# Linear attention's KV sums on 32-column tiles, and KV folded into wo on sixteen 32x32 tiles

## The chip, the cores and the metric

One core of one Trainium2 chip runs the kernel. The metric is device time in microseconds (us) of one execution. "Before" took 845.64 us (median of four runs, 845.39 to 847.52) in the rounds in which the change was timed.

Engines: PE does the matrix products (PEld is its weight load, which overlaps the products: busy 388.2 us beside PE's 838.6 in a span of 843.5), DVE is the vector engine, ACT the scalar engine, POOL the general engine, SP issues transfers (DMA). PE writes to PSUM, which this kernel uses as eight buffers of 512 f32 numbers (2 KB) a partition, called banks here; DVE and ACT copy from there.

## The reference, cut to what matters

```python
qkv = (x @ wqkv) ...                         # S = 2048, D = 1024, H = 32 heads of Dh = 32
pq, pk = phi(q), phi(k)
kv  = einsum('bhsd,bhse->bhde', pk, v)       # one 32x32 matrix a head
z   = einsum('bhsd->bhd', pk)
num = einsum('bhqd,bhde->bhqe', pq, kv)
den = einsum('bhqd,bhd->bhq', pq, z)[..., None] + 1e-06
o   = num / den
return o.transpose(...).reshape(B, S, D) @ wo
```

A layer norm with modulation stands ahead of it, and a gated MLP (D = 1024, F = 3584) follows and takes most of the time. The change touches `kv`, `z` and the product of `kv` with `wo`.

## The kernel before

Tokens go in four blocks (`sc`) of 512, each of four tiles (`t`) of 128. Four heads share one 128-column group `hg`; there are eight groups. The KV sum of block `sc-1` is taken in the middle of the K projection of block `sc`:

```python
    def kv_phase(sc):
        for hg0 in range(0, HG, 3):
            nh = min(3, HG - hg0)
            kvp = acc_b("kvp")                              # one PSUM bank
            kvv = kvp[:, 0:3 * (P + 1)].rearrange("p (g e) -> p g e", e=P + 1)
            for i in range(nh):
                for t in range(STC):
                    mm(kvv[:, i, :], lhsT=pks[sc][:, t, (hg0 + i) * P:(hg0 + i + 1) * P],
                                     rhs=vs[sc][:, t, hg0 + i, 0:P + 1], start=(t == 0), stop=(t == STC - 1))
            # DVE adds kvv to kv_acc

    for sc in range(NSC):
        if sc > 0:
            k_phase(sc, 0, 2)
            kv_phase(sc - 1)
            if sc >= 2:
                row = mod_rows(blks)                        # "modr": modulation rows, already 128x32-tiled
            k_phase(sc, 2, 4)
            # ... rest of K, V, layer norm of the next block
```

Each product is 128 by 129 (128 columns of V and a column of ones for `z`), although only the four 32x32 blocks on its diagonal are wanted. The rest is masked away, the result is transposed group by group, and wo is multiplied by it ahead of time ("fold"), so that later one product does both steps:

```python
    # after the last kv_phase: KVZ = kv_acc * kvmask (block-diagonal), Zden from z
    q_phase(1, 2, 4)
    tpk = acc_b("tp", (HG, P), BF16)
    for hg in range(HG):
        transpose(tpk[:, hg, :], KVZ[:, hg, :])
    # ... copies to KVT, den_sum(0), den_spread(0)
    q_phase(1, 4, 5)
    wf = [(hg, nb) for hg in range(HG) for nb in range(NNB)]
    for qc in range(5, 11):
        q_phase(1 + qc // 8, qc % 8, qc % 8 + 1)            # one Q chunk: 8 matmuls, then phi on ACT and DVE
        for hg, nb in wf[3 * (qc - 5):3 * (qc - 4)]:
            ps = acc_b("wf")
            w = wo[hg // 4][:, hg % 4, nb * NB:(nb + 1) * NB]
            mm(ps[:], lhsT=KVT[:, hg, :], rhs=w, start=True, stop=True)
            nc.scalar.copy(out=w, in_=ps[:])
```

PSUM is used from two pools of four banks: `acc_a` for the dense products, `acc_b` for everything else, so kvp, modr, tp, den, wf and the output projection (`a_ps`) share four banks.

## Time and profile before

| Part of PE's time | Read from | us |
|---|---|---|
| whole span of the profiled run | first line of the page | 843.5 |
| PE busy | part 1 | 838.6 |
| four KV sums | chain of waits, four pieces | 7.26 |
| fold into wo | chain of waits, six pieces | 3.47 |
| eight transposes of KV | chain of waits | 0.45 |

The page of the kernel before: the first line and part 1 give busy time and share of the span, and the last line here, from part 4, gives the shares of the chain that ended last.

```profile
span 843.5 us, 10565 instructions
...
PE 838.6 (99%) x4312; PEld 388.2 (46%) x4312; DVE 307.8 (36%) x604; ACT 173.8 (21%) x267; POOL 55.7 (7%) x160
...
PE 99%; DVE 0%; ACT 0%; issue 0%
```

PE is the bound, all the way through (busy for 99% of the span, and 99% of the chain). So only what leaves PE's stream can be gained, and whatever makes PE wait is lost.

The chain of waits of the kernel before, in order of time. Columns: start in us, length in us, what, number of instructions.

```profile
65.29 1.81 PE kvp L98 x32
...
94.73 1.81 PE kvp L98 x32
96.55 1.84 PE modr L98 x32
...
126.98 1.82 PE kvp L98 x32
128.80 1.84 PE modr L98 x32
...
158.77 1.82 PE kvp L98 x32
...
164.04 0.45 PE tp L101 x8
...
168.61 0.65 PE wf L98 x3
...
180.48 0.22 PE wf L98
```

The KV sums (kvp) take 1.81 us each, 57 ns a matmul. Two of them are followed by modr. The fold (wf) is 0.65 us for three matmuls, 216 ns each.

A piece of the chain starts with its first matmul, so the delay between kinds of matmul falls into the piece ahead of it. This delay is called the **drain** below: in the trace of the changed kernel the first matmul on smaller tiles came 93 ns late, and the first whole-array matmul after them 95 to 102 ns late (start of the next matmul, less the columns of the last). For comparisons below I use **sections**: from the end of the dense product ahead (start of its last matmul plus 216 ns) to the start of the next dense matmul. They are computed from the matmul starts in the trace.

### The profile page before, as it was taken

How to read it: one execution, taken by the hardware profiler on the slowest of the kernel's cores; microseconds unless marked ns; L12 is line 12 of the kernel's file. 1: busy time of each engine (PE TensorE's matmuls, PEld its weight loads, DVE VectorE, ACT ScalarE, POOL GpSimd, SP SyncE). 2: the span in 40 equal slices, each digit the busy share in tenths (PEclk: the TensorE clock that was granted, in tenths of full speed). 3: DMA queues.
4: the chain of work that ended last, by engine and by line, in shares of the span. 5: the costliest groups of instructions: out<-in, count | busy, mean ns of one | idle time of the engine just before them, and what ended most of it. 6: DMA issues, size and time to landing. Idle time of an engine off the chain costs nothing.

```text
span 843.5 us, 10565 instructions
## 1 busy us (share of the span) xinstructions
PE 838.6 (99%) x4312; PEld 388.2 (46%) x4312; DVE 307.8 (36%) x604; ACT 173.8 (21%) x267; POOL 55.7 (7%) x160
## 2 busy tenths in 40 slices
PE   9999999999999999999999999999999999999998
PEld 4445445544444444444444444444444444444444
DVE  5747464457433325431112344211114432111122
ACT  1454453363211110101111010011110101111000
POOL 2111010012050001100000010000000100000000
PEclk9999999999999999999999999999999999999999
DMA  9893870029989545528434073581604639720011
GB/s 302 310 260 94 246 188 1 1 52 219 348 244 266 173 142 177 169 69 268 150 101 150 19 237 95 163 279 57 200 1 118 194 69 306 238 74 0 12 64 50
DMA packets 126128, 128.74 MB, mean 153 GB/s; under 512 B 33536, under 2 KB 107776, under 8 KB 125568
## 3 DMA queue, kind: packets, MB, share of 16 engines
q1 hardware_dynamic: 122496, 115.36, 45.5%
q0 software_dynamic: 3584, 12.72, 4.8%
q8 instruction: 33, 0.54, 0.3%
q14 instruction: 15, 0.12, 0.0%
HBM read 108.01 MB, written 12.71 MB: 143 GB/s over the span
## 4 chain that ended last, share of the span: by engine, by line
PE 99%; DVE 0%; ACT 0%; issue 0%
PE acc L98 90%; PE a_ps L98 7%; PE kvp L98 1%; PE modr L98 0%; PE wf L98 0%; PE mod_ps L98 0%; PE tp L101 0%; PE den L98 0%; PE bcr L98 0%; ACT hT L220 0%; DVE hT L221 0%; PE mcol L98 0%; DVE e L593 0%; DVE ob L596 0%; DVE sel L402 0%
## 5 line engine op out<-in xcount | busy, mean ns | idle before, releaser
L98 PE MATMUL acc<-h2T,wgu 128*128 128x512 bf16 x1792 | 387.6, 379 | 0.0
L98 PEld LDWEIGHTS <-wgu 128*128 128x128 bf16 x1792 | 175.2, 98 | 211.4
L98 PE MATMUL acc<-wd,gu 128*128 128x512 bf16 (+2 forms) x924 | 196.1, 373 | 0.0
L572 DVE TENSOR_TENSOR gu<-acc,e 128x512 bf16<-128x512 f32 x112 | 77.5, 692 | 299.3 <-PE acc L98 299.3
L571 ACT ACTIVATE e<-acc 128x512 f32<-128x512 f32 x112 | 66.9, 597 | 374.8 <-PE acc L98 374.8
L98 PEld LDWEIGHTS <-gu 128*128 128x128 bf16 x924 | 89.3, 98 | 104.5
L98 PEld LDWEIGHTS <-hT 128*128 128x128 bf16 x512 | 49.6, 98 | 60.9 <-DVE hT L212 1.0
L593 DVE TENSOR_TENSOR e<-acc,gb_bc 128x512 f32<-128x512 f32 (+2 forms) x33 | 22.3, 676 | 130.1 <-PE acc L98 130.1
L98 PE MATMUL a_ps<-wo,pq 128*128 128x512 bf16 x256 | 57.4, 379 | 0.0
L98 PE MATMUL acc<-hT,wq 128*128 128x512 bf16 x256 | 57.1, 379 | 0.0
L98 PE MATMUL acc<-wk,hT 128*128 128x512 bf16 x256 | 56.9, 379 | 0.0
L98 PE MATMUL acc<-wv,hT 128*128 128x512 bf16 x256 | 55.9, 379 | 0.0
L263 ACT ACTIVATE eb<-acc 128x512 bf16<-128x512 f32 x64 | 37.9, 596 | 62.8 <-PE acc L98 58.2
L209 ACT ACTIVATE xn<-x,nmr,rstd 128x1024 bf16<-128x1024 f32 x16 | 19.8, 1240 | 126.3 <-POOL nmr L207 126.3
L264 DVE TENSOR_SCALAR eb<-eb 128x512 bf16<-128x512 bf16 x64 | 18.3, 291 | 61.2 <-ACT eb L263 61.2
L98 PEld LDWEIGHTS <-pq 128*128 128x128 bf16 x256 | 25.0, 98 | 30.2
L98 PEld LDWEIGHTS <-wq 128*128 128x128 bf16 x256 | 24.9, 98 | 29.9
L540 POOL DMA_DIRECT2D x_scratch<-x x16 | 9.6, 600 | 418.2 <-DVE x L533 418.2
L533 DVE TENSOR_TENSOR x<-a_ps,x_sb 128x512 f32<-128x512 f32 x32 | 22.1, 691 | 8.2 <-PE a_ps L98 8.1
L193 POOL TENSOR_TENSOR rstd<-veps,neg_half 128x1 f32<-128x1 f32 x32 | 18.2, 569 | 82.6 <-DVE veps L191 71.7
L301 ACT CAST v<-acc 128x512 bf16<-128x512 f32 x32 | 18.3, 582 | 22.1 <-PE acc L98 22.1
L596 DVE TENSOR_TENSOR ob<-e,x1r 128x512 bf16<-128x512 f32 (+2 forms) x33 | 22.3, 675 | 1.0
(72 smaller groups left out, 282.4 us busy)
## 6 DMA issues: line engine op xcount, KB each, us to landing
wgu<-in_B_w_gate_dram SPq DMA_DIRECT2D x28, 1024.0 KB, 7.5
wgu<-in_B_w_up_dram SPq DMA_DIRECT2D x28, 1024.0 KB, 8.7
x_sb<-in_A_x_dram SPq DMA_DIRECT2D x32, 256.0 KB, 5.8
wml<-in_w_mod_dram SPq DMA_DIRECT2D x8, 1024.0 KB, 8.3
x_scratch<-x POOLq DMA_DIRECT2D x16, 512.0 KB, 3.2
x1r<-x_scratch SPq DMA_DIRECT2D x31, 256.0 KB, 2.9
wd<-in_B_w_down_dram SPq DMA_DIRECT2D x7, 1024.0 KB, 5.6
wme<-in_w_mod_dram SPq DMA_DIRECT2D x4, 1024.0 KB, 10.5
```

Of the source, the lines that this page charges most:

```text
L98: return tc.keep_in_program_order(nc.tensor.matmul(out, lhsT=lhsT, rhs=rhs, start=start, stop=stop))
L193: nc.gpsimd.tensor_tensor(out=rstd[:, 0:n], in0=veps[:, 0:n], in1=neg_half[:].to_broadcast([P, n]), op=ALU.pow)
L209: nc.scalar.activation(out=dst, in_=src, func=ACT.Identity, bias=nmr[:], scale=rstd[:, 0:1])
L263: nc.scalar.activation(out=e[:], in_=acc, func=ACT.Exp)
L264: nc.vector.tensor_scalar(out=e[:], in0=e[:], scalar1=1.0, scalar2=PHI_EPS, op0=ALU.min, op1=ALU.add)
L301: nc.scalar.copy(out=v[:, t, nb * 4:(nb + 1) * 4, 0:P], in_=acc[:].rearrange("p (g e) -> p g e", e=P))
L533: nc.vector.tensor_tensor(out=x1[:, ns], in0=a_ps[:], in1=x_t[:, ns], op=ALU.add)
L540: nc.gpsimd.dma_start(out=x1_dram[st * P:(st + 1) * P, :], in_=x1[:])
L571: nc.scalar.activation(out=sg[:], in_=ps[0][:], func=ACT.Silu)
L572: gm = nc.vector.tensor_tensor(out=guT[sc][f // GPT][:, f % GPT, :], in0=ps[1][:], in1=sg[:], op=ALU.mult)
L593: nc.vector.tensor_tensor(out=yt, in0=y_ps, in1=gb_bc[:, ns], op=ALU.mult)
L596: nc.vector.tensor_tensor(out=ob, in0=yt, in1=x1r, op=ALU.add)
```

## The change

The intent is to stop computing the 12 of 16 blocks that are thrown away. KV is laid out as four products of 32 columns that are to run at once, each on its own 128x32 strip of PE (128 rows, 32 columns), one head each; each streams 64 columns: 32 of V, and 32 from a shared block of ones at the end of the V tile, reached by a two-piece access pattern. The fold is laid out on 16 tiles of 32x32 that are to run at once, four heads by four blocks of wo's rows, into four banks.

```diff
-        v = big("v", [STC, HG, VW])
-        nc.gpsimd.memset(v[:, :, :, P:VW], 1.0)
+        v = big("v", [VT + DH])
+        nc.gpsimd.memset(v[:, VT:], 1.0)
...
+    def v_ones(v, lo):
+        head = v[:, lo:lo + DH]
+        return bass.AP(head.tensor, head.offset, [list(head.ap[0]), [VT - lo, 2], [1, DH]])
+
     def kv_phase(sc):
-        (three groups of products of 128 x 129, three DVE adds)
+        kvp = acc_b("kvp", (HG, 2, DH))
+        for hg in range(HG):
+            for t in range(STC):
+                for i in range(HPC):
+                    mm(kvp[i * DH:(i + 1) * DH, hg, :, :], lhsT=pks[sc][:, t, hg * P + i * DH:hg * P + (i + 1) * DH],
+                       rhs=v_ones(vs[sc], t * D + hg * P + i * DH), start=(t == 0), stop=(t == STC - 1))
+        (one DVE add of 8 x 33 columns)
...
-            wo = load_w(wo_v, 0, "wo")
+            wo = [big("wo", [4, D]) for _ in range(2)]
+            for h in range(2):
+                for g in range(4):
+                    nc.sync.dma_start(out=wo[h][g * DH:(g + 1) * DH, :, :], in_=wo_v[h, g])
...
-    (mask, eight transposes)
+    (KVB = copy of kv_acc, two transposes)
...
+    def fold_wo(h, nb):
+        ns = slice(nb * NB, (nb + 1) * NB)
+        ps = [acc_b("wf") for _ in range(4)]
+        for i in range(HPC):
+            for g in range(4):
+                rs = slice(g * DH, (g + 1) * DH)
+                mm(ps[g][i * DH:(i + 1) * DH, :], lhsT=KVT[rs, h, i * DH:(i + 1) * DH], rhs=wo[h][rs, i, ns],
+                   start=True, stop=True)
+        for g in range(4):
+            (nc.scalar.copy if g % 2 == 0 else nc.vector.tensor_copy)(out=wo[h][:, g, ns], in_=ps[g][:])
+
+    q_phase(1, 4, 6)
+    fold_wo(0, 0)
+    q_phase(1, 6, 8)
+    fold_wo(0, 1)
+    q_phase(2, 0, 2)
+    fold_wo(1, 0)
+    q_phase(2, 2, 3)
+    fold_wo(1, 1)
```

More of the change, by code (lines that the diff above doesn't have):

```diff
@@ L53 @@
     FPB = FBW // P
-    VW = P + 2
+    VT = STC * D
     GPT = 8
@@ L61 @@
     wqkv_v = A_wqkv.rearrange("(c p) n -> p c n", p=P)
-    wo_v = A_wo.rearrange("(c p) n -> p c n", p=P)
+    wo_v = A_wo.rearrange("(h g i e) n -> h g e i n", h=2, g=4, i=HPC)
     wg_v = B_w_gate.rearrange("(c p) f -> p c f", p=P)
@@ L169 @@
     gb_bc = const.tile([P, D], BF16, name="gb_bc")
-    kvs = k8.tile([P, HG * VW + HG * P], F32, name="kvs", tag="k8")
-    kv_acc = kvs[:, 0:HG * VW].rearrange("p (g e) -> p g e", e=VW)
-    kvb = kvs[:, HG * VW:].bitcast(BF16).rearrange("p (k g e) -> p k g e", k=2, e=P)
-    KVZ, KVT = kvb[:, 0], kvb[:, 1]
+    kvs = k8.tile([P, HG * (2 * DH + 1)], F32, name="kvs", tag="k8")
+    kv_acc = kvs[:, 0:HG * (DH + 1)].rearrange("p (g e) -> p g e", e=DH + 1)
+    kvb = kvs[:, HG * (DH + 1):].bitcast(BF16)
+    KVB = kvb[:, 0:HG * DH].rearrange("p (g e) -> p g e", e=DH)
+    KVT = kvb[:, HG * DH:].rearrange("p (h e) -> p h e", e=P)
     Zden = const.tile([P, HG, DH], BF16, name="Zden")
-    kvmask = const.tile([P, P], BF16, name="kvmask")
     zmask = const.tile([P, HG, DH], BF16, name="zmask")
@@ L179, in build_masks @@
     def build_masks():
-        nc.gpsimd.memset(kvmask[:], 0.0)
         nc.gpsimd.memset(zmask[:], 0.0)
@@ L183, in build_masks @@
             rs = slice(h * DH, (h + 1) * DH)
-            nc.gpsimd.memset(kvmask[rs, rs], 1.0)
             for hg in range(HG):
@@ L300, in v_phase @@
                                      start=(cc == 0), stop=(cc == DC - 1))
-                nc.scalar.copy(out=v[:, t, nb * 4:(nb + 1) * 4, 0:P], in_=acc[:].rearrange("p (g e) -> p g e", e=P))
+                nc.scalar.copy(out=v[:, t * D + nb * NB:t * D + (nb + 1) * NB], in_=acc[:])
     def q_phase(sc, lo=0, hi=DC):
@@ L311, in q_phase @@
             phi_to(pqs[sc][:, qc, :], acc[:])
+    def v_ones(v, lo):
+        head = v[:, lo:lo + DH]
+        return bass.AP(head.tensor, head.offset, [list(head.ap[0]), [VT - lo, 2], [1, DH]])
     def kv_phase(sc):
-        for hg0 in range(0, HG, 3):
-            nh = min(3, HG - hg0)
-            kvp = acc_b("kvp")
-            kvv = kvp[:, 0:3 * (P + 1)].rearrange("p (g e) -> p g e", e=P + 1)
-            for i in range(nh):
-                for t in range(STC):
-                    mm(kvv[:, i, :], lhsT=pks[sc][:, t, (hg0 + i) * P:(hg0 + i + 1) * P],
-                                     rhs=vs[sc][:, t, hg0 + i, 0:P + 1], start=(t == 0), stop=(t == STC - 1))
-            dst = kv_acc[:, hg0:hg0 + nh, 0:P + 1]
-            if sc == 0:
-                nc.vector.tensor_copy(out=dst, in_=kvv[:, 0:nh, :])
-            else:
-                nc.vector.tensor_tensor(out=dst, in0=dst, in1=kvv[:, 0:nh, :], op=ALU.add)
+        kvp = acc_b("kvp", (HG, 2, DH))
[4 more added lines that the diff above has]
+                       rhs=v_ones(vs[sc], t * D + hg * P + i * DH), start=(t == 0), stop=(t == STC - 1))
+        kvv = kvp[:].rearrange("p g k e -> p g (k e)")[:, :, 0:DH + 1]
+        if sc == 0:
+            nc.vector.tensor_copy(out=kv_acc, in_=kvv)
+        else:
+            nc.vector.tensor_tensor(out=kv_acc, in0=kv_acc, in1=kvv, op=ALU.add)
     def mod_load(cols):
@@ L489 @@
     kv_phase(NSC - 1)
-    for h in range(2):
-        hs = slice(4 * h, 4 * h + 4)
-        nc.vector.tensor_tensor(out=KVZ[:, hs, :], in0=kv_acc[:, hs, 0:P],
-                                in1=kvmask[:].unsqueeze(1).to_broadcast([P, 4, P]), op=ALU.mult)
-        nc.vector.tensor_tensor(out=Zden[:, hs, :], in0=kv_acc[:, hs, P:P + 1].to_broadcast([P, 4, DH]),
-                                in1=zmask[:, hs, :], op=ALU.mult)
-    q_phase(1, 2, 4)
-    tpk = acc_b("tp", (HG, P), BF16)
-    for hg in range(HG):
-        transpose(tpk[:, hg, :], KVZ[:, hg, :])
-    nc.scalar.copy(out=KVT[:, 0:4, :], in_=tpk[:, 0:4, :])
-    nc.vector.tensor_copy(out=KVT[:, 4:8, :], in_=tpk[:, 4:8, :])
+    nc.vector.tensor_copy(out=KVB, in_=kv_acc[:, :, 0:DH])
+    nc.vector.tensor_tensor(out=Zden[:], in0=kv_acc[:, :, DH:DH + 1].to_broadcast([P, HG, DH]),
+                            in1=zmask[:], op=ALU.mult)
+    q_phase(1, 2, 4)
+    tpk = acc_b("tp", (2, P), BF16)
+    for h in range(2):
+        transpose(tpk[:, h, :], KVB[:, 4 * h:4 * h + 4, :].rearrange("p g e -> p (g e)"))
+    nc.vector.tensor_copy(out=KVT, in_=tpk[:])
     den_sum(0)
     den_spread(0)
-    q_phase(1, 4, 5)
-    wf = [(hg, nb) for hg in range(HG) for nb in range(NNB)]
-    for qc in range(5, 11):
-        q_phase(1 + qc // 8, qc % 8, qc % 8 + 1)
-        for hg, nb in wf[3 * (qc - 5):3 * (qc - 4)]:
-            ps = acc_b("wf")
-            w = wo[hg // 4][:, hg % 4, nb * NB:(nb + 1) * NB]
-            mm(ps[:], lhsT=KVT[:, hg, :], rhs=w, start=True, stop=True)
-            nc.scalar.copy(out=w, in_=ps[:])
+    def fold_wo(h, nb):
[16 more added lines that the diff above has]
+    fold_wo(1, 1)
     h2Ts = {}
```

## The prediction

> **What bounds the kernel.** TensorE (PE): busy 838.6 of 843.5 us (99%) in the profile's first part, full clock in every slice. The chain that ended last is 99% PE; DVE and ACT have under 2 us of it.
>
> **What is touched, on the chain of waits:**
> - KV sums: four pieces of 1.81 to 1.82 us, 32 matmuls each, 7.26 us. In the timeline they start 56 ns apart: 129 columns streamed over the whole array.
> - Fold into wo: 16 matmuls of 512 columns, 216 ns apart: 3.47 us.
> - Eight transposes of the masked KV: 0.45 us; two remain (0.11): -0.34 us.
>
> **What tiles cost.** This trace's denominator product is already 128x32-tiled: four matmuls start within about 10 ns, the next four 56 ns later, the time of 128 columns on the whole array. So four column tiles run at once, weight loads hidden, steadily over 96 matmuls. PE starts about 94 ns late going in and 105 ns late coming out: 0.2 us a round trip. [...]
>
> **KV after.** 128 matmuls a phase, 64 columns (32 of V, 32 ones), four at a time: 32 groups. Streaming alone would be about 29 ns a group; weight loads and the issue of eight instructions must fit too, and are shown only to fit in 56. Estimate 33 ns: 1.06 us a phase. Two of four phases are followed by the modulation rows, already 128x32-tiled, so two round trips are new (0.4 us). Saving 4 x 0.75 - 0.4 = 2.6 us (-0.4 at 56 ns, 3.1 at 29).
>
> **Fold after.** Four folds of 16 tiles 32x32 into four PSUM banks. If all 16 run at once: 216 ns + about 60 for issue + 0.2 drain, 0.48 us each, 1.9 in all: saves 1.55. [...] no record of this trace shows row tiles. If row groups serialise, 4.2 us: loses 0.7.
>
> **Off the chain, near zero:** fewer DVE accumulates, no mask multiply, half of the wf copies (605 ns each) moved from ACT to DVE, where Q's phi takes 1.0 us of each 1.73 us chunk: they fit.
>
> **A new wait.** wo is loaded by eight transfers instead of two, on the queue that also issues the hT transposes of the last token block. An issue took 0.5 to 0.9 us, so those may come up to 1.8 us later; the modulation before the last K phase had about 0.9 us of slack. I allow 0.5 us of PE wait near 122 us.
>
> **Prediction.** 2.6 + 1.55 + 0.34 - 0.5 = 4.0 us less: 841.9 us, range 840.3 to 845.2. That is 0.5%: faster by over 2% 1%, within 2% 98%, slower 1%.
>
> **What would show it.** KV pieces of 1.0 to 1.2 us in the chain, groups of four 29 to 36 ns apart; folds under 0.5 us with 16 starts within about 70 ns; transposes 0.11 us; den, modr and dense products unchanged; a DVE hT piece on the chain before the last K phase if the queue delays it.
>
> **What would make it wrong.** Groups at 45 ns or more (weight load or issue binds, or the two-piece pattern reads slowly); row tiles serialising; larger drains at 32x32; wo's transfers stalling PE by over a microsecond.

The 0.2 us a round trip is read from the trace of the kernel before (93 ns in, 105 out). The 33 ns a KV group is my estimate, between 29 (64 of 129 columns that took 57) and 56, and so are the 60 ns for the issue of a fold (four starts within about 10 ns make some 50 for sixteen). That 16 tiles of 32x32 run at once was assumed: the trace of the kernel before doesn't show it.

## The result, and the profile after

The changed kernel took 843.96 us (median of four, 843.62 to 844.47) against 845.64. The ratio is 0.9976 (95% interval 0.9959 to 0.9993). Ratios here are the mean time of one kernel's fast runs over that of the other's of the same rounds, so not quite the ratio of the medians. A second set of rounds gave 843.20 against 845.69, ratio 0.9973. So about 2 us were gained, half of the 4.0 forecast.

The page of the changed kernel, the lines that answer to those of before:

```profile
span 842.5 us, 11410 instructions
...
PE 835.4 (99%) x4738; PEld 383.7 (46%) x4738; DVE 308.0 (37%) x602; ACT 169.6 (20%) x258; POOL 54.8 (7%) x155
...
PE 98%; DVE 1%; DMA 0%; issue 0%; ACT 0%; SPq 0%
```

PE is still the bound; it has 3.2 us less to do, but the span is only 1.0 us shorter in this pair of runs. The chain of waits of the changed kernel, same columns ("issue" is time in which the engine waited for nothing that the profile shows):

```profile
65.94 1.15 PE kvp L98 x128
...
94.83 1.15 PE kvp L98 x128
95.98 1.73 PE modr L98 x32
...
126.31 1.15 PE kvp L98 x128
127.46 1.50 PE modr L98 x26
128.96 1.59 issue
130.55 0.61 PE modr L98 x6
...
159.29 1.15 PE kvp L98 x128
...
164.00 0.11 PE tp L101 x2
...
168.24 0.36 PE wf L98 x16
...
172.16 0.36 PE wf L98 x16
...
177.77 1.21 DVE wo L513 x2
...
179.02 0.43 PE wf L98 x13
```

The KV pieces went from 1.81 to 1.15 us, four times the same. The folds are 0.36 us each, the transposes 0.11. But in the third KV section a new piece stands: 26 of modr's 32 matmuls are done, then PE does nothing for 1.59 us and the profile knows no reason. And the last fold has a piece of DVE ahead of it. Groups of the changed kernel by shape show the same (busy us, mean ns of one, then idle us just before them and what ended it):

```profile
L98 PE MATMUL kvp<-v,pk 128*32 128x64 bf16 x512 | 4.9, 197 | 0.0
...
L98 PE MATMUL modr<-wml,sc 128*32 128x512 bf16 x64 | 4.2, 380 | 1.6 <-issue 1.6
...
L98 PE MATMUL wf<-wo,kvs 32*32 32x512 bf16 x64 | 2.3, 384 | 0.2 <-DVE wo L513 0.2
```

Set out by section (us):

| Section | before | changed | difference |
|---|---|---|---|
| first KV | 1.814 | 1.246 | -0.57 |
| second KV and modr | 3.751 | 2.978 | -0.77 |
| third KV and modr | 3.751 | 4.948 | +1.20 |
| fourth KV | 1.816 | 1.248 | -0.57 |
| transposes and first den | 1.103 | 0.767 | -0.34 |
| fold into wo | 3.453 | 0.460, 0.460, 0.459, 1.263 | -0.81 |
| other small products (bcr, mcol, late den) | 2.815 | 2.816 | 0 |
| sum | 18.503 | 16.645 | -1.86 |

The sum agrees with the measured 2 us (0.6 to 3.5 us by the interval of the ratio). Had the third KV section cost what the second did (1.97 us less) and the last fold what the others did (0.80 less), the gain would have been 4.6 us. So the question of the experiments is what these two waits are.

One thing must be kept out of it. The time from the start to the first KV section ("head") is 65.13 us in the first trace of before and 65.78 in this one, although no PE instruction differs there. In this profiled run the clock record has a stretch of 3.41 us at half speed, at 24.4 us, in which matmuls start 427 ns apart instead of 216; the mean granted clock is 0.998. Over all the traces the head was 64.3 to 65.2 us where the clock record has no such stretch (a second trace of before: 64.73; of the changed kernel: 64.69) and 65.8 to 66.2 where it has one. Runs of either kind count as fast. That is why differences under a microsecond are read from the sections below, not from times.

### The profile page after: what moved, and what is told of

It reads as the page before. It is cut to its first block, busy times and chain, and to the rows that moved or that the text cites. A ratio compares the mean times of both kernels' runs of the same rounds, so it can differ in the third digit from the quotient of the medians.

```text
span 842.5 us, 11410 instructions
## 1 busy us (share of the span) xinstructions
PE 835.4 (99%) x4738; PEld 383.7 (46%) x4738; DVE 308.0 (37%) x602; ACT 169.6 (20%) x258; POOL 54.8 (7%) x155
## 4 chain that ended last, share of the span: by engine, by line
PE 98%; DVE 1%; DMA 0%; issue 0%; ACT 0%; SPq 0%
PE acc L98 89%; PE a_ps L98 7%; PE kvp L98 1%; PE modr L98 0%; DVE stats L197 0%; DMA x_sb<-in_A_x_dram 0%; PE mod_ps L98 0%; PE den L98 0%; PE tp L101 0%; DVE wo L513 0%; PE wf L98 0%; DVE xn L201 0%; PE bcr L98 0%; DVE pq L264 0%; ACT eb L261 0%
## 5 line engine op out<-in xcount | busy, mean ns | idle before, releaser
L98 PE MATMUL acc<-wk,hT 128*128 128x512 bf16 x256 | 58.6, 387 | 0.0
```

The lines of the kernel that those rows point to most:

```text
L98: return tc.keep_in_program_order(nc.tensor.matmul(out, lhsT=lhsT, rhs=rhs, start=start, stop=stop))
```

## The experiments

Two theories about the pause of the third KV section stood against each other at first. **Mine:** PE had no instructions. The changed KV phase has 256 PE instructions (a weight load and a matmul, 128 times) where it had 64, and goes through them in 1.15 us; the page's part 3 lists a queue q8 with packets that only carry instructions:

```profile
q8 instruction: 33, 0.54, 0.3%
```
```profile
q8 instruction: 37, 0.61, 0.3%
```

The first line is of the kernel before, the second of the changed one (packets, MB, share of the DMA engines). The trace has the single packets: all are of 16 KB, and in the long dense stretch one comes, on average, every 256 PE instructions (128 pairs, about 27.6 us). **Rivals:** the weights of the modulation rows (wml), whose median landing time went from 8.3 to 9.9 us, came late; or PE needs the time to recover from 128 small matmuls. The traces already speak against the first rival: in the changed kernel the last of these weights landed at 106.9 us, 20 us before the modr that pauses, and the same median of 9.9 us stands in the page of e_fold (below), which has no pause.

For the last fold: it waits for PSUM banks which DVE has yet to copy out (mine), or it is slow by itself.

### One half at a time

**The KV part alone** (e_kv), with the fold as before:

```diff
# against the changed kernel, put in short
+    KVZ[:, :, js] = kv_acc[:, :, 0:DH] * kvmask[:, js]   for each of 4 column blocks js
+    wo load, eight transposes, wf loop as in the kernel before
```

> The KV part alone: 128x32 KV tiles as in the changed kernel, the fold into wo as before (block-diagonal KV rebuilt with the mask, 16 whole-array matmuls). Section times are PE time from the end of the dense product ahead to the start of the next one. My theory: KV sections 1.25, 2.98 and 1.25 us, and the third one (KV and modulation rows) near 4.9 us, because PE runs dry of instructions there for about 2 us (same instruction count ahead of it as in the changed kernel). Fold and transposes as before (3.45 and 1.10 us with den). Net against before: 2 x 0.57 + 0.77 - 1.2 = about 0.7 us faster, 845.0. Rival (the late wml transfers of the changed kernel's schedule make the stall): the same stall, so this run doesn't tell the two apart; it tells how much of the gain KV keeps.

Measured: 843.66 us against 845.75, ratio 0.9975 (0.996 to 0.999). Sections 1.25, 2.98, 3.98 and 1.25; folds and transposes as before. The pause is there, but it costs the section 1.01 us (3.98 for 2.98), not the 1.97 of the changed kernel. So the KV part is worth 1.68 us of section time even with its pause, and the size of the pause differs from one run to another.

**The fold part alone** (e_fold), with KV as before:

```diff
# against the changed kernel, put in short
-    v_ones, kv_phase on 32-column tiles
+    v_phase, kv_phase as in the kernel before
+    KVB[rs_i] = kv_acc[rs_i, :, rs_i]                    for each of 4 partition blocks rs_i
```

> The fold part alone: KV as before, 32x32-tiled fold and two transposes as in the changed kernel. My theory: no stall at the third KV section (3.75 us as before); folds 0.46, 0.46, 0.46 us, the last near 1.26 us because it comes one Q chunk after the third and waits for two PSUM banks that DVE has not yet copied out; transposes and den 0.77 us. Net 3.45 + 1.10 - 2.64 - 0.77 = 1.1 us faster than before, about 844.5. If the last fold's wait belongs to the tiles themselves, all four would be above 0.6.

Measured: 843.46 us against 845.75, ratio 0.9979 (0.9964 to 0.9994). KV sections as before (1.82, 3.75, 3.75, 1.82), no pause; folds 0.46, 0.46, 0.46 and 1.26. By sections the fold part gives 1.14 us. The two halves add up: 1.68 + 1.14 = 2.82, and the changed kernel's 1.86 is less by 0.96, which is what its pause was longer than that of the KV part alone. (The medians say 2.1 and 2.3 us, with intervals over 2 us wide; the heads of runs without a trace are not known.)

### Does the pause sit at a transfer or at a place in the instruction stream?

Only matmuls in the warm-up at the start are exchanged here. There PE multiplies zeros while it waits for the first tokens (in the trace of the kernel before these matmuls start about 427 ns apart at first, and 216 ns apart from 7.06 us on). The edit shifts every later PE instruction by a known count and changes nothing else.

```diff
# e_shift72: 72 places; e_shift128: keep_warm 20 and 70 small ones, 128 places
-    keep_warm(accs[5], 26)
+    keep_warm(accs[5], 23)
+    for _ in range(39):
+        mm(accs[5][:, 0:1], lhsT=sel[:, 0, :], rhs=sel[:, 0, 0:1], start=True, stop=True)
```

> As the run with 128 places, but shifted by 72 (3 wide warm-up matmuls out, 39 one-column ones in), which puts a block's end at about the same place in the second KV burst as it had in the third. My theory: the pause moves: second KV section (with its modulation rows) between 4 and 5 us, third back to 2.98 us; time as the changed kernel, about 844.0. Rivals: third section stays 4.9 us, second 2.98.

Measured: 843.13 us against 845.75, ratio 0.997 (0.9955 to 0.9985). The chain of waits of this run:

```profile
64.48 1.15 PE kvp L98 x128
...
93.36 1.15 PE kvp L98 x128
94.51 1.50 PE modr L98 x26
96.01 1.18 issue
97.19 0.61 PE modr L98 x6
...
126.39 1.15 PE kvp L98 x128
127.54 1.73 PE modr L98 x32
```

The pause (96.01, issue) has moved into the second KV section, by 31 us, and the third is clean: 2.98 us. No transfer was moved to do that. Its first KV section is of use too: it holds a block end at the same place, 52 instructions in, and is followed by dense matmuls instead of modr. It has no pause (1.25 us).

The shift by 128 places (e_shift128) was expected to do this:

> The changed kernel, with 64 more matmuls in the warm-up at the head (6 wide ones out, 70 one-column ones in), nothing else. That moves every later PE instruction by 128 places against the 256-instruction (16 KB) blocks in which the trace shows PE's instructions being fetched. My theory (PE ran out of fetched instructions at the third KV section): the pause of 1.76 us is gone, third KV section 2.98 us, no other pause, 2.0 us faster than the changed kernel, 842.0. Rival 1 (weights of the modulation rows or another transfer landed late): the section stays at 4.9 us. Rival 2 (the drain or the queue after a burst of 128 small matmuls): it stays too.

Measured: 845.28 us against 845.75, ratio 0.9993 (0.9976 to 1.001). The forecast of 842.0 us and of no other pause was a miss. The pause did leave the third section (2.98 us), but two new ones came, in the first (2.17 us) and the second (4.85 us):

```profile
66.04 1.14 PE kvp L98 x127
67.18 0.73 issue
67.91 0.20 PE kvp L98
...
95.85 1.14 PE kvp L98 x126
96.98 1.68 issue
98.67 0.21 PE kvp L98 x2
```

Here PE stops with one and with two of 128 KV matmuls to go, at the end of an accumulation whose operands have been in use for a microsecond. That too speaks against late data and against a recovery after the burst. I had reckoned only with a block end early in a burst; with a block end just ahead of a burst, the next falls on its last instructions.

The decisive reading is the place of every pause, counted in PE instructions (two a matmul) from the start, beside the instruction packet that ended last ahead of its end. From the traces (us):

```
kernel             last start   next start   place   mod 256   packet from   to
changed              128.577      130.549     2236      188      128.090    129.128
changed, again       127.485      129.314     2236      188      126.975    128.086
KV alone             127.322      128.330     2236      188      126.003    126.949
34 columns           128.909      130.535     2236      188      128.140    129.180
late last fold       127.855      129.959     2236      188      127.542    128.582
shift 72              95.632       97.186     1724      188       94.821     95.940
shift 128             66.985       67.912     1214      190       65.410     66.522
shift 128             96.784       98.665     1724      188       96.296     97.351
```

In eight pauses out of eight, in seven traces, PE stops at the same remainder of 256 (one pair later in one case), whatever it is computing, and goes on 1.23 to 1.42 us after the end of a 16 KB instruction packet. I read the pause as PE waiting for its next block of 256 instructions. No view shows what PE holds, but of the theories here this one alone fits all eight, and the rivals fall. In the changed kernel the third KV section starts at instruction 1928, so blocks end 52 instructions into the burst and again 256 later, inside modr; all 320 instructions of the two are due within 2.9 us. In the second section, from 1344, the block end after the one in the burst lies at 1724, among dense matmuls of 108 ns an instruction and 8.9 us after the other, and there was no pause (2.98 us).

The packet itself took 0.95 to 1.12 us, and from its start to PE's next matmul it took 2.3 to 2.5 us in all eight; but the start itself varied, so that the pause at one place (2236) cost its section 1.0 to 2.1 us. At that place the packet started 0.83 us (KV alone) to 1.84 us (late last fold) after PE had begun the 256 instructions that end there, and the costs of the five traces stand in the same order as these delays. What sets the delay is not settled. One more thing can be counted in the traces: in the eight cases PE got from one block end to the next within 1.5 to 2.2 us; the closest two block ends without a pause lay 3.2 us apart (third section of e_shift72). How many blocks PE holds was not measured.

### Why a KV phase takes 1.15 us and not 0.93

In the changed kernel the first nine groups of four KV matmuls start 29 ns apart, which is about what 64 columns take (129 took 57 ns); after that single matmuls start 8.3 ns apart, 33 ns a group. The test (e_n34) streams 34 columns instead of 64:

```diff
-        ... [VT - lo, 2], [1, DH]
+        ... [VT - lo, 2], [1, 17]
```

> The changed kernel with KV matmuls of 34 streamed columns (two pieces of 17) in place of 64; the result is wrong on purpose. In the changed kernel the first nine groups of four go 29 ns apart and then single matmuls start 8.3 ns apart. My theory: from there PE is bound by the issue of a weight load and a matmul each 8.3 ns, not by columns: the first and last KV sections stay at 1.20 to 1.25 us, starts 8.3 ns apart. Rival (columns bind, or reading the two-piece pattern): the time falls with the columns, to about 0.73 us a section. The pause at the third section stays near PE instruction 2236, as the instruction count is the same.

Measured, one look: result wrong as meant; first and last KV section 1.22 us, second 2.97, third 4.59 with the pause at 2236. After the first eight groups single matmuls start 8.3 ns apart again. So with about half the columns 0.03 us a section is gained: from there on a weight load and a matmul go every 8.3 ns with 34 columns as with 64. Neither weight loads as such nor the two-piece pattern set it: from the second to the eighth group the starts here were about 25 ns apart, 6 ns a pair. I take the 8.3 ns to be the rate at which PE gets through instructions; no view shows its queue, so this name for it is argued and not shown. On the whole array no such pace was seen: in the trace of the kernel before, one-column matmuls (mod_ps) start 25 ns apart.

### The last fold

```diff
     q_phase(2, 2, 3)
-    fold_wo(1, 1)
...
     q_phase(2, 3, 4)
+    fold_wo(1, 1)
     with tc.issue_after(last_phi[0].ins):
         den_apply(0)
```

> The changed kernel with the last fold one Q chunk later, two chunks after the third fold as the others have it; nothing else. My theory (the last fold waits for two PSUM banks whose copies stand on DVE behind phi): the last fold section falls from 1.26 to 0.46 us, all else as the changed kernel, 0.8 us faster than it. Rival (the last fold is slow by its own data or bank order): stays 1.26 us.

In the changed kernel's timeline (start, length, engine, line, what, and in brackets idle time before and what ended it) the last fold stops after three of its matmuls until DVE has copied the banks of the third fold; the two copies stand behind phi on DVE:

```profile
177.08 0.69 DVE L264 SCALAR_TENSOR_TENSOR pq<-acc,eb 128x512 bf16<-128x512 f32 x1
177.69 1.28 DVE L513 CAST wo<-wf 128x512 bf16<-128x512 f32 x2
...
178.21 0.58 PE L98 MATMUL wf<-wo,kvs 32*32 32x512 bf16 x3
...
179.02 0.43 PE L98 MATMUL wf<-wo,kvs 32*32 32x512 bf16 x13 [0.23 <-DVE wo L513]
```

With the fold one chunk later, the chain of waits of e_foldlate has equal pieces for all four (the second is left out):

```profile
167.64 0.36 PE wf L98 x16
...
175.49 0.36 PE wf L98 x16
...
179.41 0.36 PE wf L98 x16
```

The last section fell from 1.263 to 0.459 us. The time was 843.61 against 845.43 (ratio 0.9977), no visible gain over the changed kernel. With an interval of 2.8 us a gain of 0.8 could not be seen in times anyway, and the trace shows two losses beside it: the pause of the third KV section was 0.13 us longer in it, and the later copies pushed the denominator multiply on DVE back, so that the first output-projection matmuls waited in two gaps, 0.28 us in all. Of 0.80 us, 0.52 remain once these gaps are counted.

### A version with half the instructions

If instructions bind, use fewer. Here pairs of heads run on two 128x64 tiles, 64 matmuls of 65 columns a phase (64 of V, one of ones); half of the product is again thrown away, which cost nothing here (a KV piece of 1.14 us for 1.15), with 65 columns streamed at once for 64.

```diff
# against the changed kernel; last fold late as above; PW = 2 * DH
-        v = big("v", [VT + DH])
+        v = big("v", [STC, 2 * HG, PW + 1])
...
+        for g0 in range(0, HG, 4):
+            kvp = acc_b("kvp", (4, PW + 1))
+            for g in range(4):
+                for t in range(STC):
+                    for k in range(2):
+                        c = 2 * (g0 + g) + k
+                        mm(kvp[k * PW:(k + 1) * PW, g, :], lhsT=pks[sc][:, t, c * PW:(c + 1) * PW],
+                           rhs=vs[sc][:, t, c, :], start=(t == 0), stop=(t == STC - 1))
+            (DVE adds kvp to kv_acc)
...
+    KVB[rs_i] = kv_acc[rs_i, :, (i % 2) * DH:(i % 2 + 1) * DH]     for each of 4 partition blocks
```

> Head pairs on two 128x64 tiles in place of heads on four 128x32 tiles: 64 KV matmuls of 65 columns a phase instead of 128 of 64, half the PE instructions; the two diagonal blocks are picked when KV is copied out at the end; last fold one chunk later. My theory: groups of two about 29.6 ns apart without the issue limit, KV sections 1.14 us alone and about 3.0 with the modulation rows (a further drain between 64- and 32-column tiles allowed for), no pause for instructions anywhere, as 128 plus 64 instructions are less than one block of 256; last fold 0.46. Sections sum 13.7 us against 18.5 before and 16.6 changed: 4.8 us faster than before, about 840.9. Rival (pauses come from something other than instruction fetch): a pause near 2 us at the third section remains.

Measured: correct, 842.06 us against 845.43, ratio 0.9957 (0.9942 to 0.9972). Its chain of waits:

```profile
65.19 1.14 PE kvp L98 x64
...
94.06 1.14 PE kvp L98 x64
95.20 1.84 PE modr L98 x32
...
125.64 1.14 PE kvp L98 x64
126.78 1.84 PE modr L98 x32
...
177.46 0.36 PE wf L98 x16
```

No pause in any section. The sections sum to 14.05 us, 4.45 less than before. Two expectations were too good: a group of two took about 32 ns, not 29.6, so the KV section is 1.24 us and no shorter than with 32-column tiles, and the drain between 64- and 32-column tiles ahead of modr costs 0.1 us (3.08 for 2.98 us). Against the changed kernel the sections gain 2.60 us: 1.97 by the pause that doesn't come and 0.80 by the later fold, less 0.2 for the two drains; nothing by faster matmuls. The two gaps of 0.28 us at the output projection are here too.

**The repeat** (e_best) was to take these gaps away by putting the last fold's copies behind the denominator multiply:

```diff
     q_phase(2, 3, 4)
-    fold_wo(1, 1)
     with tc.issue_after(last_phi[0].ins):
         den_apply(0)
+    fold_wo(1, 1)
```

> Head pairs on 128x64 tiles and the last fold one chunk later, as in the earlier run of pairs, with the last fold's copies put behind the denominator multiply on DVE, which in that run made the first output-projection matmuls wait 0.28 us in two gaps. Expected: no such gaps, no pause, sections 14.05 us in all, 841.7 us: about 2 us faster than the changed kernel and 3.7 faster than before.

Measured: 841.63 us against 845.69, ratio 0.9947 (0.9934 to 0.996), but the gaps are still there: a comparison of the two builds shows the same instructions in the same order on every engine. The edit did nothing, so the run counts as a second run of the same kernel. On the same chip the **changed kernel again** took 843.20, somewhat less than expected:

> The changed kernel as it is, for a second trace and for times on the same chip as the run beside it: 843.6 to 844.2 us. If the pause is one of instruction fetch it stands again at PE instruction 2236 (third KV section), though its length may differ (0.8 to 1.9 us in the traces so far); last fold 1.26 us again.

Its pause stood at 2236 again (third section 4.81 us), and its last fold took 1.262 us. Of its six runs four took 842.44 to 843.22 with a granted clock of 1.000, and two 844.76 and 845.85 with 0.998. So pairs on 64-column tiles with the last fold later beat both kernels, by 1.6 and 4.1 us in these medians.

### The kernel before again

> The kernel before, unchanged, for a second trace of it: sections as in its first trace (18.5 us in all), and the head up to the first KV section anywhere between 64.3 and 66 us, depending on where the half-speed clock stretches fall. If the head is again near 65.1 while kernels with the change show 64.3 to 64.5 where the clock has no dip, the head is part of the difference; if it varies as much as theirs, it is not.

845.38 us, sections 18.503 us in all, the same to the third decimal as in the first trace; head 64.73. The heads of changed kernels without the half-speed stretch were 64.31 to 65.19. They overlap, so nothing here makes the head a part of what the change does.

## Why the prediction was right or wrong

The forecast was 841.9 us, range 840.3 to 845.2; the measured 843.96 lies in it, nearer to its upper end: a gain of about 2 us for one of 4.0. Point by point:

- **"PE is the bound, only its stream counts"**: right. In every run with an interval the section sums (less the 0.28 us of gaps where they stand) agree with the time within it; the DVE, ACT and POOL work that was saved shows in no time.
- **KV, "2.6 us"**: right in size. Without the pause the four sections fell by 2.68 us (3.63 to 2.49 for the two alone, 7.50 to 5.96 for the two with modr). A group took 29 and then 33 ns for 33 assumed, and the piece 1.15 us. The reason hinted at was right as well: instructions, not columns (e_n34). But 33 was picked between 29 and 56 and worked out from nothing, so that it hit so closely is luck.
- **The drain, "0.2 us a round trip"**: right. In the changed kernel a KV section starts 93 ns late and ends about 101 ns late, a fold the same.
- **Fold, "0.48 us each, 1.9 in all: saves 1.55"**: right for three of four (0.46). All 16 tiles ran at once: their matmuls started within 50 ns in each of the three, and a fold took 0.46 us with its drains, where 16 of 216 ns one after another would take 3.46 us (an estimate from this trace). The step that failed is "half of the wf copies (605 ns each) moved from ACT to DVE ...: they fit". They fit where two chunks stand between folds; the last fold has one, and four banks in use twice made PE wait for DVE: 0.80 us.
- **"A new wait ... I allow 0.5 us of PE wait near 122 us"**, by wo's eight transfers: wrong. The chain of the changed kernel has no hT piece ahead of the third KV section; the dense stretch there is 24.17 us, as before. The order on the queue was not as assumed: only one of wo's eight transfers stands ahead of the last three hT transposes (109.99 us; so did one of two before), and the other seven are issued behind them, from 116.13 us.
- **What was missing**: the 426 extra matmuls are 852 extra PE instructions, and they have to arrive: q8 brought 37 packets of 16 KB for 33. The prediction asked whether eight instructions a group can be *issued* in 29 ns, and not whether they had *arrived*. That cost 1.97 us, the largest of the misses, and e_shift72 and e_shift128 show it by moving it. The page of the kernel before lists the queue (q8, 33 packets); the prediction made no use of it.

In sum: 4.5 us of predicted savings were 4.6 us in fact, 0.5 us of predicted waiting were 2.8 us, and none of that at the place that was named. That the time still fell into the range is luck in this respect: the range left room for slower groups and for wo's wait, which did not come, and two other waits took up that room.

## What to carry to other kernels

Splitting a product into tiles multiplies PE's instructions for the same work (128 matmuls a KV phase for 32 here), so count instructions as well as columns: in this kernel pairs on column tiles came no faster than 8.3 ns for long, and where two ends of 256-instruction blocks fell within 2.2 us PE stopped, at a cost of up to 2.1 us and at a place that shifts with any change in the number of instructions ahead of it. When PE idles and the profile names no cause, count instructions up to the pause in two builds; if the place stays the same modulo 256, as in these eight cases, look for fewer and larger matmuls: half of them took the pause away (e_pair64_late). Dense work behind the burst is no sure help: the first section of e_shift72 had no pause with it, that of e_shift128 one that cost 0.92 us. And a step that takes all banks of a PSUM pool at once needs its copies done before it comes round again (0.80 us in the last fold): check the shortest distance between two of them, not the usual one.
